# Attention and two MLPs on one core: zero products ahead of the loop, an earlier load of v, six score buffers, and where the weight conversion stands

## The chip, the cores and the metric

The kernel runs on one core of one Trainium2 chip. The core has TensorE (PE; PEld is its weight load), VectorE (DVE), ScalarE (ACT), GpSimd (POOL) and SyncE (SP, which here only issues transfers). The metric is device time in microseconds (us), lower is better. Of three runs of the kernel before the median is 755.74 us (747.38 to 756.08).

## The reference

Attention over two batches ("halves" b = 0 and 1), 12 heads, 448 tokens, with a 12x12 mixing of the heads before and after the softmax, and behind it two MLPs on all 896 tokens.

```python
scores = scale * np.matmul(q, k.transpose(0, 1, 3, 2))
scores = np.einsum('bhij,hg->bgij', scores, w_pre)
attn = np.exp(scores - np.max(scores, axis=-1, keepdims=True))
attn = attn / (np.sum(attn, axis=-1, keepdims=True) + 1e-09)
attn = np.einsum('bhij,hg->bgij', attn, w_post)
x = np.matmul(attn, v)            # to (896, 768)
x = ((x @ w_a) * (x @ w_b)) @ moe_w_out
out = np.maximum(x @ w_in, 0.0) ** 2 @ moe2_w_out
```

All of it is in fp32; `moe_` and `moe2_` weights are 768x1536, 1536x768, 768x2048 and 2048x768.

## The kernel before

The 448 query rows of a half are cut into four tiles of 120, 120, 120 and 88 rows (`tiles`, t = 0 to 3), eight tiles in all. For each pair of heads c = 0 to 5 a tile's scores are made on TensorE by `qk` (L188, products at L201), copied from PSUM (`qk_copy`, L208: odd heads on VectorE, even heads on ScalarE), and each head's copy is spread by a transfer (`spread`, L215, mostly issued on SP) into `G`, in which the 12 heads of a query row lie on neighbouring partitions. There are two `G`, one for even and one for odd t. From the third tile on the copies land in `s` buffers, four of them before (L113); a buffer is free again when the spread that reads it has landed.

The loop (L705) runs over 46 slots. A slot takes one or two groups of ten query rows (`PAIRS`); tiles have 6, 6, 6, 5, 6, 6, 6 and 5 slots, so tiles begin at slots 0, 6, 12, 18, 23, 29, 35 and 41 (`base`). In slot n TensorE mixes the heads of slot n+1 (`premix`, L287, T from G), then does the second mixing of slot n (`post`, L336). The softmax of n+1 is a minimum on VectorE (L296), an exponential on ScalarE (L303) and, in `weights2`, three small VectorE steps (L315 to L317) that fold 1/sum into the weights of `post`. `evac` (L353 VectorE, L355 ScalarE) copies the result of `post` into `a`. In the last slot of a tile the product with v follows (`av`, L367, six head pairs in three thirds; each third is copied by `av_out`, L377, on VectorE).

Everything else is put into slots by lists: `mid`, `end`, `pre`, `aft` and `dve_l` hold calls by slot. The scores of the next tile are called in six successive slots from three before the current tile's start. The load of v for half two (`load_v`, 1344 KB) is called at slot 20. A weight unit is 768 columns of 128 rows, 68 units in all; it is loaded on SP (`load_w`, L489) and converted in six steps, s0 to s5 (L497 to L532): s0 to s3 on VectorE (L503, L507, L514, L518; s0 with a ScalarE step, L502), s4 on ScalarE (L524), and s5 the low part, on GpSimd for units 0 and 1 (`lower`, L163) and on VectorE for the rest (L531). Eighteen steps, three units, are called one by one in slots 31 to 42 through `dve_l`, right behind `weights2`.

In front of the loop the scores of tile 0 are made and spread, even heads from GpSimd's queue and odd heads from SP's (`hw`, L406; `first_out`, L418); the first slot has a path of its own (`direct`). Nine products with a zero column (`busy`, L396) fill the time in which the first inputs load. Behind the loop the dense part (`stage`, L594) does the MLPs, three products per 128x128 block of weights. Its first 11 block steps are called inside slots 41 to 45 (`fill`).

Of the kernel before, what the change touches and what calls it, by code (L numbers as in the profile page):

```python
# [40 lines left out]
R0 = 2 * ND  # L41
# [27 lines left out]
def attention_moe_kernel(  # L69
# [22 lines left out]
    def rd(ap):  # L92
        return ap.bitcast(F32)
# [18 lines left out]
    sb = att.enter_context(tc.tile_pool(name="att", bufs=1))  # L112
    s_p = att.enter_context(tc.tile_pool(name="s", bufs=4))  # L113
    e_p = att.enter_context(tc.tile_pool(name="e", bufs=2))
# [303 lines left out]
    def first_out():  # L418
        while Sps:
            _, t, h, p = Sps.pop(0)  # L420
            qk_copy(ROWS0, h, p, stage0[h])
            spread(0, h, stage0[h], R0, H, hw[h % 2])

# [14 lines left out]
    NS = len(plist)  # L438
    dve_l, pre, aft, mid, end = {}, {}, {}, {}, {}

    def at(d, slot, *f):
        d.setdefault(max(slot, 0), []).append(f)
# [5 lines left out]
    for ti, (b, t) in enumerate(tiles):  # L448
        s0, sp = base[ti], span[ti]
        if ti + 1 < len(tiles):  # L450
            nxt = tiles[ti + 1]
            for c in range(NC):
                if ti:
                    at(mid, s0 - 3 + c, qk, *nxt, c)
# [15 lines left out]
        if ti + 1 < len(tiles):  # L470
            for c in range(NC):
                at(end, s0 + sp - 1, av, b, t, c)
                if c % 2:
                    at(end, s0 + sp - 1, av_out, b, t, c // 2)
        if t == 1 and b + 1 < B:
            at(mid, s0 + sp + 8, load_v, b + 1)

# [4 lines left out]
    whl = {}  # L482
    todo = []

# [9 lines left out]
    def split_steps(u):  # L494
# [31 lines left out]
        def s5():  # L526
            lo = w_p.tile([128, UW], F32R, tag="wl", name="wl", bufs=3)
            if u < 2:
                lower(lo, st["c"], st["hi"], 6)
            else:  # L530
                nc.vector.tensor_tensor(out=lo, in0=st["c"], in1=rd(st["hi"]), op=ALU.subtract)  # L531
            whl[u] = (st["hi"], lo)  # L532
# [3 lines left out]
    def split_w(u):  # L536
        if u < NU:
            todo.extend(split_steps(u))

    def steps(n):  # L540
        for _ in range(min(n, len(todo))):
            todo.pop(0)()

# [16 lines left out]
    s1 = base[-2]  # L560
    at(mid, s1 - 8, load_w, 0)
    at(mid, s1 - 8, load_w, 1)
    for u in range(3):
        at(mid, s1 - 5, split_w, u)
    for i in range(18):
        at(dve_l, s1 - 4 + (2 * i) // 3, steps, 1)
    for c in range(NC):
# [130 lines left out]

    premix(*plist[0])
    softmax(0)  # L700
    qk(0, 1, 0)
# [3 lines left out]
    for n in range(NS):  # L705
# [12 lines left out]
        if n + 1 < NS:  # L718
            weights2(*plist[n + 1])
        run(dve_l, n)  # L720
        run(mid, n)
# [116 lines left out]
```

## Time and profile before

| | |
|---|---|
| median of 3 runs | 755.74 us (747.38 to 756.08) |
| the profiled execution | 758.59 us, span 756.8 us |
| its mean granted TensorE clock | 0.979 |
| TensorE busy | 728.2 us, 96% of the span |
| VectorE, ScalarE, GpSimd busy | 483.7, 309.5, 83.0 us |
| HBM read | 62.29 MB, 86 GB/s over the span |

The profile was taken in one execution of its own. All times in its rows are us from the start of the span. A row of the order in time gives the start, the busy time of a merged run of instructions, the engine, the line, the operation, what it writes and reads, and in brackets how long the engine was idle before and what ended that. The granted clock is a share of 2.4 GHz.

### The profile page before, as it was taken

The page shows a single profiled execution, that of the slowest core. Times are in us where ns is not written, and L with a number is a line of the kernel's source. Part 1 is how long each engine was busy: PE and PEld are TensorE (multiplying, and loading weights), DVE is VectorE, ACT ScalarE, POOL GpSimd, SP SyncE. Part 2 cuts the span into 40 slices and gives each one's busy share as a digit, 9 for nine tenths or more (in the row PEclk, how much of TensorE's full clock was granted, in tenths as well). Part 3 has the DMA queues.
Part 4 walks back from the last instruction along what each step waited for, and adds up shares of the span by engine and source line. Part 5 has one row for each costly group of instructions (what it writes and reads, how often), then busy time and mean ns, then how long its engine had stood idle before and what let it go on. Part 6 is the DMA issues. An engine that isn't in the chain of part 4 may idle for free.

```text
span 756.8 us, 13175 instructions
## 1 busy us (share of the span) xinstructions
PE 728.2 (96%) x5309; PEld 611.4 (81%) x5309; DVE 483.7 (64%) x820; ACT 309.5 (41%) x581; POOL 83.0 (11%) x181
## 2 busy tenths in 40 slices
PE   8799996999989999999999999999999999999998
PEld 2466773776667899999999999999999999999997
DVE  6467664568665576676667755656888888544440
ACT  3358644546544433333333333324555554332220
POOL 4126721102840000000000000000000000000000
PEclk9799998899979999999999999999999999999999
DMA  7564336263310133323322332332232323443410
GB/s 231 147 187 147 107 102 186 73 212 129 109 61 2 43 122 101 112 84 126 123 86 92 121 121 84 126 123 86 85 126 85 124 90 120 149 147 112 134 40 25
DMA packets 27451, 84.75 MB, mean 112 GB/s; under 512 B 4422, under 2 KB 16890, under 8 KB 27166
## 3 DMA queue, kind: packets, MB, share of 16 engines
q1 hardware_dynamic: 24286, 80.08, 32.3%
q0 software_dynamic: 2528, 2.75, 1.4%
q10 hardware_dynamic: 576, 1.07, 0.4%
q8 instruction: 42, 0.69, 0.4%
q14 instruction: 19, 0.16, 0.1%
HBM read 62.29 MB, written 2.75 MB: 86 GB/s over the span
## 4 chain that ended last, share of the span: by engine, by line
PE 83%; DMA 6%; DVE 3%; issue 3%; POOL 2%; ACT 2%; SPq 0%; DVEq 0%; ACTq 0%; POOLq 0%
PE T L574 8%; PE T L575 8%; PE T L573 8%; PE post L336 6%; PE qk L573 6%; PE post L575 6%; PE post L573 6%; PE post L574 6%; PE qk L575 5%; PE qk L574 5%; DMA G<-s 4%; PE av L367 3%; PE T L287 3%; PE av L575 3%; PE av L574 3%; PE av L573 3%
## 5 line engine op out<-in xcount | busy, mean ns | idle before, releaser
L336 PEld LDWEIGHTS post<-w,e 64*112 64x112 f32 x1440 | 80.9, 182 | 36.0 <-issue 21.9
L524 ACT CAST wh<-wc 128x768 fp32r<-128x768 f32 x68 | 56.8, 835 | 121.8 <-DVE wc L518 108.8
L531 DVE TENSOR_TENSOR wl<-wc,wh 128x768 fp32r<-128x768 f32 x66 | 63.0, 955 | 49.6 <-ACT wh L524 49.6
L336 PE MATMUL post<-w,e 64*112 64x60 f32 x1440 | 86.2, 268 | 4.5 <-DVE w L317 4.1
L303 ACT ACTIVATE e<-T,nb 128x448 f32<-128x448 f32 (+1 forms) x92 | 57.5, 630 | 77.4 <-DVE nb L296 77.4
L574 PE MATMUL T<-m,wh 128*128 128x448 f32 x213 | 78.5, 368 | 0.2 <-DVE m L549 0.2
L573 PE MATMUL T<-m,wh 128*128 128x448 f32 x213 | 78.5, 368 | 0.0
L575 PE MATMUL T<-m,wl 128*128 128x448 f32 x213 | 78.4, 368 | 0.0
L507 DVE SCALAR_TENSOR_TENSOR wa<-wr,wa 128x768 uint32<-128x768 uint32 x68 | 65.3, 961 | 2.3
L518 DVE SCALAR_TENSOR_TENSOR wc<-wc,wa 128x768 uint32<-128x768 uint32 x68 | 65.2, 958 | 2.2
L287 PE MATMUL T<-G,wpre_sb 64*64 64x448 f32 x352 | 49.8, 587 | 12.4 <-DMA G<-s 7.0
L502 ACT ACTIVATE wc<-wr 128x768 f32<-128x768 f32 x68 | 61.6, 906 | 0.0
L296 DVE TENSOR_REDUCE nb<-T 128x1 f32<-128x448 f32 (+1 forms) x92 | 52.9, 615 | 13.4 <-PE T L287 13.0
L514 DVE TENSOR_SCALAR wc<-wc 128x768 f32<-128x768 f32 x68 | 37.7, 555 | 16.6 <-ACT wc L502 16.6
L573 PE MATMUL post<-m,wh 128*128 128x448 f32 x125 | 46.0, 368 | 0.0
L574 PE MATMUL post<-m,wh 128*128 128x448 f32 x125 | 46.0, 368 | 0.0
L575 PE MATMUL post<-m,wl 128*128 128x448 f32 x125 | 46.0, 368 | 0.0
L353 DVE COPY a<-post 112x480 f32<-112x480 f32 x44 | 30.1, 684 | 24.9 <-PE post L336 24.9
L574 PEld LDWEIGHTS T<-m,wh 128*128 128x128 f32 x213 | 40.0, 188 | 4.6 <-DVE m L549 0.5
L573 PEld LDWEIGHTS T<-m,wh 128*128 128x128 f32 x213 | 40.0, 188 | 4.3 <-ACT m L548 0.3
L575 PEld LDWEIGHTS T<-m,wl 128*128 128x128 f32 x213 | 40.0, 188 | 4.0
L573 PE MATMUL qk<-m,wh 128*128 128x448 f32 x116 | 42.7, 368 | 0.0
(163 smaller groups left out, 1454.1 us busy)
## 6 DMA issues: line engine op xcount, KB each, us to landing
wr<-w SPq DMA_DIRECT2D x68, 768.0 KB
G<-s SPq DMA_DIRECT2D x44, 210.0 KB
G<-s SPq DMA_DIRECT2D x22, 140.0 KB
k<-kT SPq DMA_DIRECT2D x12, 224.0 KB
v<-v SPq DMA_DIRECT2D x2, 1344.0 KB
outT<-ta SPq DMA_DIRECT2D x12, 224.0 KB
q<-qT SPq DMA_DIRECT2D x6, 360.0 KB
G<-x POOLq DMA_DIRECT2D x6, 175.0 KB, 5.4
```

The source lines that it names most:

```text
L287: nc.tensor.matmul(p[f][o:o + 64, 0:S], wpre_sb[i:i + 64, o:o + 64], G[t % 2][i:i + 64, r + g, :], start=True, stop=True, skip_group_check ...
L296: nc.vector.tensor_reduce(out=NB[b, m][0:q, f:f + 1], in_=Tps[b, m][f][0:q, 0:S], op=ALU.min, axis=AX.X)
L303: nc.scalar.activation(out=e[0:q], in_=Tps[b, m][f][0:q, 0:S], func=ACTF.Exp, bias=NB[b, m][0:q, f:f + 1], scale=-1.0, accum_out=Z[b, m][0 ...
L336: nc.tensor.matmul(p[g][0:JP, c:c + k], e[o:o + 64, j * JP:(j + 1) * JP], w2[o:o + 64, f, :], start=True, stop=True,)
L502: nc.scalar.activation(out=st["c"], in_=rd(st["high"]), func=ACTF.Abs, scale=HSC)
L507: nc.vector.scalar_tensor_tensor(out=a, in0=st["high"], scalar=0x80000000, in1=a, op0=ALU.bitwise_and, op1=ALU.bitwise_or)
L518: nc.vector.scalar_tensor_tensor(out=cu, in0=cu, scalar=3, in1=st["a"], op0=ALU.logical_shift_left, op1=ALU.bitwise_or)
L524: nc.scalar.copy(st["hi"], st["c"])
L531: nc.vector.tensor_tensor(out=lo, in0=st["c"], in1=rd(st["hi"]), op=ALU.subtract)
L573: nc.tensor.matmul(p[:, 0:S], hi[:, sl], x[0], start=first, stop=False)
L574: nc.tensor.matmul(p[:, 0:S], hi[:, sl], x[1], start=False, stop=False)
L575: nc.tensor.matmul(p[:, 0:S], lo[:, sl], x[0], start=False, stop=last)
```

## The change

- `busy(16)` is called between `premix` and `softmax` of the first slot: 16 more zero products.
- In front, the spreads of heads 8 and 10 of tile 0 are issued by ScalarE and not by GpSimd.
- `s` has six buffers and not four.
- `load_v` for half two moves from slot 20 to slot 17 (the last slot of a tile).
- Of the scores of half two's first tile, head pair 3 moves to the end of slot 17, behind the product with v, and pairs 4 and 5 follow one slot sooner (slots 18 and 19).
- `dve_l` is gone. The weight steps are called at slots 28, 34 and 40 only, between the thirds of the product with v: 2+2, 2+2+3 and 2+2+1 steps (`STEPS`); the last two of the eighteen come in `attention_tail`. Units 0 and 1 are loaded at slots 22 and 28 (both at 27 before). The low part of units 0 and 1 is made by VectorE.

```diff
-    s_p = att.enter_context(tc.tile_pool(name="s", bufs=4))
+    s_p = att.enter_context(tc.tile_pool(name="s", bufs=6))
...
-            spread(0, h, stage0[h], R0, H, hw[h % 2])
+            spread(0, h, stage0[h], R0, H, nc.scalar if h in (8, 10) else hw[h % 2])
...
+    STEPS = ((2, 2, 0), (2, 2, 3), (2, 2, 1))
...
-                if ti:
+                if ti == 3:
+                    if c != 3:
+                        at(mid, s0 - 3 + c - (c > 3), qk, *nxt, c)
+                elif ti:
                     at(mid, s0 - 3 + c, qk, *nxt, c)
...
                 if c % 2:
+                    if b:
+                        at(end, s0 + sp - 1, steps, STEPS[t][c // 2])
                     at(end, s0 + sp - 1, av_out, b, t, c // 2)
-        if t == 1 and b + 1 < B:
-            at(mid, s0 + sp + 8, load_v, b + 1)
+        if ti == 2:
+            at(end, s0 + sp - 1, qk, *tiles[4], 3)
+        if t == 2 and b + 1 < B:
+            at(mid, s0 + sp - 1, load_v, b + 1)
...
-            if u < 2:
-                lower(lo, st["c"], st["hi"], 6)
-            else:
-                nc.vector.tensor_tensor(out=lo, in0=st["c"], in1=rd(st["hi"]), op=ALU.subtract)
+            nc.vector.tensor_tensor(out=lo, in0=st["c"], in1=rd(st["hi"]), op=ALU.subtract)
...
-    at(mid, s1 - 8, load_w, 0)
-    at(mid, s1 - 8, load_w, 1)
+    at(mid, base[4] - 1, load_w, 0)
+    at(mid, base[5] - 1, load_w, 1)
     for u in range(3):
-        at(mid, s1 - 5, split_w, u)
-    for i in range(18):
-        at(dve_l, s1 - 4 + (2 * i) // 3, steps, 1)
+        at(mid, base[5] - 1, split_w, u)
...
     premix(*plist[0])
+    busy(16)
     softmax(0)
```

ScalarE's order in front of the loop, where the copies of the last heads of tile 0 stand (`x` are the copies, `G_83` is the `G` of even tiles, x_1_122 and x_2_123 are heads 8 and 10):

```order
 L266 COPY s<-T 128x448
 L212 COPY x_1_122<-qk 100x448
+L220 DMA G_83<-x_1_122 10x10x448
 L212 COPY x_2_123<-post 100x448
+L220 DMA G_83<-x_2_123 10x10x448
 L303 ACTIVATE e,z<-T,nb 128x448 x2
 L212 COPY v_124<-qk 120x448
```

The two transfers now stand on ScalarE between the copies and the first exponentials; they were in GpSimd's queue.

SP's queue around the spreads of half two's first tile and of the tile after it (`G_83` and `G_84` are the two `G`; `wr` is a weight unit):

```order
 L220 DMA G_83<-s 10x12x448 x2
 L140 DMA q<-qT 128x720
-L220 DMA G_83<-s 10x12x448 x8
+L220 DMA G_83<-s 10x12x448 x2
 L184 DMA v<-v 112x3072
-L220 DMA G_83<-s 10x12x448
+L220 DMA G_83<-s 10x12x448 x7
 L220 DMA G_83<-s 9x12x448
 L223 DMA G_83<-s 1x12x448
 L220 DMA G_84<-s 10x12x448 x2
 L140 DMA q<-qT 128x720
```

The load of v stood behind ten of the tile's spreads and stands behind four now.

VectorE's order in slot 28, the last slot of half two's first tile. Before:

```order
L317 TENSOR_TENSOR w_2093<-wp,z 128x120
L210 COPY s<-qk 120x448
L377 COPY x_0_2124<-av 128x2x120
L377 COPY x_1_2143<-post 128x2x120
L377 COPY x_2_2162<-av 128x2x120
L296 TENSOR_REDUCE nb<-T 128x1 x2
```

With the change (L516, L520, L527 and L531 of the changed kernel are L503, L507, L514 and L518 before):

```order
L317 TENSOR_TENSOR w_2108<-wp,z 128x120
L210 COPY s<-qk 120x448
L516 TENSOR_SCALAR wa<-wr 128x768
L520 SCALAR_TENSOR_TENSOR wa<-wr,wa 128x768
L377 COPY x_0_2148<-av 128x2x120
L527 TENSOR_SCALAR wc<-wc 128x768
L531 SCALAR_TENSOR_TENSOR wc<-wc,wa 128x768
L377 COPY x_1_2169<-post 128x2x120
L377 COPY x_2_2188<-av 128x2x120
L296 TENSOR_REDUCE nb<-T 128x1 x2
```

The first four steps of unit 0 came between the product with v and its copies; in slots 31 to 33, where they stood behind L317, they are gone.

## Rows read from the trace of the kernel before

**Rows 1.** Busy time by stretch: engines (instructions), clock, DMA share, GB/s.
```profile
20.00:30.00 10.00, 7.10 (x46) 4.71 (x48) 2.09 (x4) 2.13 (x6) 0.78 (x2) 0.61 0.46 123
130.00:140.00 10.00, 10.00 (x104) 7.92 (x104) 2.88 (x8) 2.88 (x7) 0.00 (x0) 0.59 0.33 104
220.00:230.00 10.00, 9.06 (x108) 8.03 (x106) 2.88 (x8) 1.17 (x4) 0.00 (x0) 0.65 0.20 75
290.00:300.00 10.00, 10.00 (x50) 9.09 (x49) 7.34 (x11) 3.29 (x6) 0.00 (x0) 1.00 0.26 80
```

**Rows 2.** Order in time, slots 17 to 23: start, busy, engine, line, idle before.
```profile
100.53 0.53 ACT L212 COPY s<-qk 120x448 f32<-120x448 f32 x1 [1.36 <-DMA G<-s]
...
108.87 1.78 PE L336 MATMUL post<-w,e 64*112 64x60 f32 x32
...
115.49 1.78 PE L336 MATMUL post<-w,e 64*112 64x60 f32 x32
...
117.90 0.49 SPq L184 DMA_DIRECT2D v<-v  x1
...
121.12 1.79 PE L336 MATMUL post<-w,e 64*112 64x60 f32 x32
...
129.74 2.12 PE L287 MATMUL T<-G,wpre_sb 64*64 64x448 f32 x8 [6.17 <-DMA G<-s]
...
131.79 2.87 PE L336 MATMUL post<-w,e 64*112 64x60 f32 x14
...
141.87 1.78 PE L336 MATMUL post<-w,e 64*112 64x60 f32 x32
```

**Rows 3.** Order in time, slots 32 to 41.
```profile
177.51 1.78 PE L336 MATMUL post<-w,e 64*112 64x60 f32 x32
...
190.18 1.86 PE L367 MATMUL av<-a,v 112*64 112x120 f32 x32 [0.93 <-ACT a L355]
...
193.73 0.41 DVE L377 COPY x<-post 128x240 f32<-128x240 f32 x1 [1.23 <-PE post L367]
...
195.25 0.98 PE L287 MATMUL T<-G,wpre_sb 64*64 64x448 f32 x8
...
214.79 1.59 DVE L315 TENSOR_SCALAR z<-z 128x2 f32<-128x2 f32 x1
...
221.22 3.47 PE L367 MATMUL av<-a,v 112*64 112x120 f32 x32 [0.94 <-ACT a L355]
...
229.09 0.98 PE L287 MATMUL T<-G,wpre_sb 64*64 64x448 f32 x8
...
231.43 1.78 PE L336 MATMUL post<-w,e 64*112 64x60 f32 x32
```

**Rows 4.** Order in time, front: zero products, first wait, first and third `post`.
```profile
0.93 3.52 PE L399 MATMUL av<-warm 128*1 128x448 f16 x9 [0.93 <-DVE warm L381]
...
22.90 2.03 PE L287 MATMUL T<-G,wpre_sb 64*64 64x448 f32 x8 [4.66 <-DMA G<-x]
...
26.50 3.11 PE L336 MATMUL post<-w,e 64*112 64x60 f32 x32
...
36.86 1.78 PE L336 MATMUL post<-w,e 64*112 64x60 f32 x32
```

**Rows 5.** Order in time: the first two VectorE steps of a weight unit.
```profile
177.29 0.55 DVE L503 TENSOR_SCALAR wa<-wr 128x768 uint32<-128x768 uint32 x1
...
177.88 0.96 DVE L507 SCALAR_TENSOR_TENSOR wa<-wr,wa 128x768 uint32<-128x768 uint32 x1
```

**Rows 6.** The chain of work that ended last: start, us, what.
```profile
15.72 7.05 DMA G<-x
...
35.22 0.80 PE qk L201 x4
...
139.81 1.21 PE av L367 x32
```

**Rows 7.** The page's DMA issues: count, KB each, median us to landing.
```profile
G<-x POOLq DMA_DIRECT2D x6, 175.0 KB, 5.4
```

More of the change, by code (lines that the diff above doesn't have):

```diff
@@ L438, in attention_moe_kernel, with steps @@
     NS = len(plist)
-    dve_l, pre, aft, mid, end = {}, {}, {}, {}, {}
+    pre, aft, mid, end = {}, {}, {}, {}
+    STEPS = ((2, 2, 0), (2, 2, 3), (2, 2, 1))
+    todo = []
+    def steps(n):
+        for _ in range(min(n, len(todo))):
+            todo.pop(0)()
     def at(d, slot, *f):
@@ L482, in attention_moe_kernel @@
     whl = {}
-    todo = []
     def load_w(u):
@@ L538, in split_w @@
             todo.extend(split_steps(u))
-    def steps(n):
-        for _ in range(min(n, len(todo))):
-            todo.pop(0)()
     xs = [[None] * NC for _ in range(B)]
@@ L719, in attention_moe_kernel @@
             weights2(*plist[n + 1])
-        run(dve_l, n)
         run(mid, n)
```

## The prediction

> **What bounds the kernel now.** I read the table by stretch first [rows 1]. From about 253 us to the end TensorE is busy 10.00 us of every 10 at the full granted clock (1.00, 2.4 GHz), with VectorE at some 7: the reader sees one row of it, and the rows up to 740 us are like it. This is the dense part; the change does not touch its products, so its 504 us stay. Everything to be won lies in the 253 us of attention. There the table has three bad stretches, 20 to 30 us (clock 0.61), 130 to 140 (0.59, behind a long wait) and 220 to 230 (0.65). In each the clock has fallen to its lower level, 1.2 GHz, after TensorE had little to do.
>
> Next I read the order in time. One trip of the loop, a slot, runs from one `post` product (L336) to the next, so the starts of L336 give the length of each slot. An undisturbed slot takes 3.3 us (108.87 to 115.49 is two of them) [rows 2]. A slot that ends a tile also holds the product with v, and takes about 8.7: 1.78 for `post`, 0.9 for scores, 5.07 for the product (190.18 to 195.25), 0.98 for the next mixing product [rows 3]. Lengths above these are the loss, and they lie in three places.
>
> Front: TensorE has done the scores of tile 1 that it can at 18.24 and waits 4.66 us for the spread of scores into `G`; the eight products behind that wait take 2.03 us, against 0.98 later [rows 3, 4]. Middle: slots 20 to 22, 115.49 to 141.87, in which a `G<-s` transfer behind the 1.3 MB load of v ends a wait of 6.17 us [rows 2]. End of attention: slots 32 to 40, 177.51 to 231.43, where the steps of weight conversion stand in VectorE's queue between one slot's softmax and the next [rows 3, 5].
>
> **The change, part by part.** The sum is made against the profiled execution, 758.59 us with a span of 756.8; the median of the runs shown is 755.74, 2.85 below it.
>
> *Front.* Sixteen zero products go in behind the first mixing product. Nine of them took 3.52 us at half clock, 0.39 each [rows 4]; the trace has none at full clock, so the price lies between 0.39 each (6.3 us in all) and half of it (3.1). I take 3.1, since the clock stood at 1.00 where they go; half clock was seen only after the wait. They start at 16.5 and end near 19.6, and the two score products that now follow them (0.8 to 1.0 each [rows 6]) end near 21.6. The wait is then filled to within 1.3 us, if `G` comes when it did. It was ended by a spread issued on SP at 15.72 that took 7.05 us to land, while tile 1's first four spreads were already under way [rows 6]. These now start 3 us later, and the spreads of heads 8 and 10 leave POOL's queue (5.4 us to landing [rows 7]) for ACT's. So I take `G` to be there at about 21.5. ACT issues two more transfers ahead of its exponentials, some 0.8 us each by SP's spreads; the first `post` comes 3 us after these are done, so that is covered. At full clock the slots then run: mixing 0.98 and scores 0.85, `post` at 23.4 instead of 26.50; two further slots of 4.8 (with two score products each waiting for the copies of the one before) and 3.6 us, so the third `post` at 31.8 instead of 36.86 [rows 4]. **Front: 5.0 us saved.** If `G` comes no sooner than 22.90, 3.7. If the zero products don't hold the clock, they only delay scores that nobody waits for yet: 0. Above, if `G` lands by 20.5, the score products still end at 21.6, so 5.3.
>
> The Trainium skill, DMA: Bandwidth & Descriptors, section "Issuing engines are not separate DMA queues", says that the queues of SP, ACT and POOL feed the same 16 DMA engines. By it heads 8 and 10 would land no sooner for leaving POOL, and the front would save the 3.7 and not the 5.0; no row of the kernel before has a spread on ACT's queue, so this stays open.
>
> *Middle.* Two things move. The load of v goes from slot 20, where SP issued it at 117.90 among the last spreads of the tile, to slot 17, whose product with v gives its transfer 5 us in which few others are due. And the scores of heads 6 and 7 are made one slot sooner, so the last spread leaves in slot 20 and not in 21, two slots ahead of the mixing product that reads it. That product then has no wait: slot 20 shrinks from 5.63 to 3.3, slot 21 from 10.67 to 3.3, and slot 22 (half a `post`, the 88-row product with v at 1.21 for each third [rows 6], full clock) from 10.08 to 6.8: 12.98 saved [rows 2]. The moved score product costs slot 17 its 0.85. Six `s` buffers let the copies run three score products ahead of the landing; ACT's wait of 1.36 us for `G<-s` in slot 17 [rows 2] is one of two in a row on the chain there, and I count 1.2 for them. **Middle: 13.0 - 0.85 + 1.2 = 13.4.** Bounds: 6 if the load now delays the spreads of slots 17 and 18 by its own 5 us and half the wait comes back; 14.5 at best. What is queued behind the load on SP are those spreads, and who waits for them is the copy three score products later.
>
> *End of attention.* In slots 31 to 42 eighteen steps leave VectorE's queue between softmaxes. A unit costs VectorE 0.55 and 0.96 in its first pair of steps [rows 5], two instructions of the same shape again, and one such for the low part: some 4 us. They now stand between the thirds of the product with v in slots 28, 34 and 40, where VectorE waits 1.23 us before each copy of 0.41 [rows 3]. Cover: a window of 5.07 us, less three copies of 0.41 and one of 0.62, leaves 3.2 for the 3.0 of steps in slot 28; slot 34 has 4.0 for the 3.2, and overruns by 0.8, of which the next mixing product (0.98) and `post` hide most. The low parts of two units go from POOL to VectorE, 0.96 each, inside the 4.0. Two steps are left for the last product with v; the dense part has 25 product triples before it reads that unit. So the nine slots 32 to 40 become seven of 3.4 (the casts of x stay), one of 8.8, and the last: 1.78, 0.9 of wait for a copy, 5.07, and 2.34 from its mixing product to the next `post` (229.09 to 231.43), 10.1 [rows 3]. That is 42.7 against 53.92: **11.2 saved**; the half clock of 217 to 227 us is in it. Bounds: 8 if all three windows overrun by 1 us; 13 if the slots go at 3.3 and overrun nothing.
>
> A row beside it: z's step on two columns took 1.59 us at 214.79, while POOL subtracted [rows 3]. The Trainium skill, SBUF — State Buffer, section "Who interferes with whom", says that the one of the two engines that comes second to their shared port blocks fully until the other is done. By it, the POOL subtractions of x that stay could still block such steps, and if that took 0.3 in each of six slots the end would save 9.4; the row agrees, but it stands beside a POOL subtraction of weights, which goes.
>
> **Sum:** 5.0 + 13.4 + 11.2 = 29.6, so 758.6 - 29.6 = 729.0 for a profiled execution; the unprofiled runs of the kernel before stand 2.85 lower, which gives 726.2. I say 727.
>
> **The rivals.**
> 1. *The load of v only moves its collision.* Spreads of slots 17 and 18 land 5 us late and stop the copies in spite of six buffers; the middle saves 6 and not 13.4: 734. For it: 6.17 us of wait followed this very load. Against: in slot 17 the product with v goes on for 5 us in which no copy is due.
> 2. *The clock falls at another place.* Half speed made 3.47 us of a third of the product with v at 221.22, which takes 1.86 at 190.18 [rows 3]; over such a fall that is 4 to 5 us: 732. Against: all three falls followed a wait or thin slots that go away.
> 3. *The steps overrun, and `G` is late in front.* VectorE late by 1 us in each window (end 8.2), zero products without effect (front 0): 735.
> 4. *Little comes.* Front 0, middle 6, end 8: 741.7, within 2%. It needs three lower bounds at once.
> 5. *Slower.* Unit 2 is finished only in the tail. If the line of units stays one behind through the dense part, TensorE waits at each of its 68 units: 0.44 us a unit eats the 29.6, and from 0.65 (44 us, 771) the kernel is slower by 2%. Against: VectorE is busy only 7 of 10 us there [rows 1], so it catches up within a few units.
>
> **How the numbers follow.** Forecast with all three savings near their size: 0.64, own range 721 to 733. Rival 1: 0.12; rival 2: 0.10; rival 3: 0.07; rival 4: 0.05; rival 5: 0.02. The range takes in the best bounds (5.3 + 14.5 + 13 = 32.8, so 723, and a little more for the offset of 2.85) and rivals 1 to 3 above: 720 to 736. A measurement of this kernel can tell about 2% from no change, 15 us: faster than 740.6 are the forecast and rivals 1 to 3, 0.93; within 2% rival 4 and half of rival 5, 0.06; slower 0.01.
>
> **What would show it.** Right: granted clock 1.00 in all stretches from 10 to 240 us; the first `post` of the loop near 23.4; no wait above 1 us for `G<-s` near 110 us; slots 29 to 40 at 3.3 to 3.5 us except where the product with v stands; the dense part from about 223. Wrong: a fall of the clock at 20 us, a wait of TensorE in the middle of the product with v in slots 28, 34 and 40, or waits for `wl` after the start of the dense part.

## The result

The changed kernel takes 721.23 us (median of four runs, 719.91 to 725.20) against 755.91 us before (747.38 to 757.57); the ratio is 0.9572, 95% interval 0.9490 to 0.9653. It is faster, as forecast, and the forecast of 727 lies 5.8 us above it. Two errors of opposite sign make that small difference, and the sections below are about them. The profiled execution of before, 758.59 us, is one of the longer ones of its kernel (747.38 to 757.57 in the other four).

The profiled execution of the changed kernel takes 725.20 us, with a span of 723.4. Its table by stretch, with the columns of [rows 1] (engines' busy time, clock, DMA share, GB/s):

```profile
20.00:30.00 10.00, 10.00 (x104) 5.82 (x103) 6.68 (x16) 5.69 (x15) 2.84 (x5) 1.00 0.56 147
...
40.00:50.00 10.00, 7.88 (x101) 5.78 (x99) 5.01 (x14) 5.09 (x14) 3.11 (x8) 0.91 0.75 214
...
130.00:140.00 10.00, 9.95 (x140) 6.80 (x141) 8.30 (x21) 7.58 (x19) 2.43 (x6) 1.00 0.29 87
...
220.00:230.00 10.00, 9.97 (x156) 8.81 (x154) 3.05 (x8) 3.22 (x9) 0.00 (x0) 1.00 0.01 2
```

The three bad stretches of before, at clocks of 0.61, 0.59 and 0.65, are at 1.00. A new one has come, 40 to 60 us (0.91 in its first half, 0.92 in its second). TensorE's order in time shows where it comes from (start, busy, line, idle before):

```profile
17.65 3.22 PE L399 MATMUL av<-warm 128*1 128x448 f16 x16
...
22.49 0.98 PE L287 MATMUL T<-G,wpre_sb 64*64 64x448 f32 x8
...
24.25 1.69 PE L336 MATMUL post<-w,e 64*112 64x60 f32 x32
...
32.05 1.78 PE L336 MATMUL post<-w,e 64*112 64x60 f32 x32
...
47.07 2.40 PE L367 MATMUL av<-a,v 112*64 112x120 f32 x32 [1.88 <-DMA v<-v]
49.19 3.04 PE L367 MATMUL post<-a,v 112*64 112x120 f32 x32
```

Against [rows 4], the wait of 4.66 us in front is gone, sixteen zero products took 3.22 us, and the third `post` starts at 32.05 instead of 36.86. Then, at 47.07, the product with v waits 1.88 us for the load of half one's v; the clock falls, and its second third takes 3.04 us where such a third takes 1.81 to 1.86 elsewhere.

The middle and the end of attention, in the same view:

```profile
114.59 1.78 PE L336 MATMUL post<-w,e 64*112 64x60 f32 x32
...
121.69 0.98 PE L287 MATMUL T<-G,wpre_sb 64*64 64x448 f32 x6 [0.32 <-DMA G<-s]
122.60 1.58 PE L336 MATMUL post<-w,e 64*112 64x60 f32 x14
...
129.88 1.29 PE L336 MATMUL post<-w,e 64*112 64x60 f32 x22
...
165.39 1.78 PE L336 MATMUL post<-w,e 64*112 64x60 f32 x32
...
200.30 1.86 PE L367 MATMUL av<-a,v 112*64 112x120 f32 x32 [0.88 <-DVE z L315]
...
207.70 1.49 PE L336 MATMUL post<-w,e 64*112 64x60 f32 x26
```

The wait of 6.17 us for `G<-s` [rows 2] has become 0.32 in this trace, and slots 32 to 40 run from 165.39 to 207.70, 42.31 us, instead of 53.92 [rows 3].

Starts of `post` (L336) cut each trace into the same stretches. Before and after were both profiled a second time, on one chip (the runs e_before and e_after below), and the table has all four traces, in us:

| stretch | before, 1st | after, 1st | saved | before, 2nd | after, 2nd | saved |
|---|---|---|---|---|---|---|
| start to slot 6 | 55.73 | 54.71 | 1.02 | 52.76 | 51.73 | 1.03 |
| slots 6 to 15 | 39.72 | 39.96 | -0.24 | 39.46 | 40.34 | -0.88 |
| slots 16 to 23 | 49.74 | 38.54 | 11.20 | 51.79 | 37.36 | 14.43 |
| slots 24 to 31 | 32.32 | 32.18 | 0.14 | 32.20 | 32.18 | 0.02 |
| slots 32 to 40 | 53.92 | 42.31 | 11.61 | 52.79 | 42.31 | 10.48 |
| slot 41 to the end | 525.37 | 515.70 | 9.67 | 515.70 | 515.68 | 0.02 |
| span | 756.8 | 723.4 | 33.4 | 744.7 | 719.6 | 25.1 |

Three lines were not foreseen: the first, where only 1.0 of the 4.8 us won by the third `post` is left; the second, where the changed kernel loses (0.24 and 0.88); and the last but one, where the first pair of traces shows 9.67 us that the second does not.

### The profile page after: what moved, and what is told of

The parts are those of the page before. It is cut to its first block, busy times and chain, and to the rows that moved or that the text cites. A ratio compares the mean times of both kernels' runs of the same rounds, so it can differ in the third digit from the quotient of the medians.

```text
span 723.4 us, 13184 instructions
## 1 busy us (share of the span) xinstructions
PE 708.0 (98%) x5325; PEld 604.4 (84%) x5325; DVE 482.8 (67%) x822; ACT 309.1 (43%) x581; POOL 76.9 (11%) x167
## 4 chain that ended last, share of the span: by engine, by line
PE 88%; DMA 4%; POOL 2%; DVE 2%; issue 2%; ACT 1%; SPq 0%; DVEq 0%; ACTq 0%; POOLq 0%
PE T L578 9%; PE T L579 9%; PE T L577 9%; PE post L336 7%; PE qk L577 6%; PE post L577 6%; PE post L579 6%; PE post L578 6%; PE qk L579 6%; PE qk L578 6%; PE T L287 4%; PE av L367 3%; PE av L577 3%; PE av L578 3%; PE av L579 3%; PE qk L201 2%
## 5 line engine op out<-in xcount | busy, mean ns | idle before, releaser
L336 PEld LDWEIGHTS post<-w,e 64*112 64x112 f32 x1440 | 76.9, 175 | 32.8 <-issue 14.0
L541 DVE TENSOR_TENSOR wl<-wc,wh 128x768 fp32r<-128x768 f32 x68 | 65.3, 960 | 48.5 <-ACT wh L537 48.5
L336 PE MATMUL post<-w,e 64*112 64x60 f32 x1440 | 82.1, 260 | 2.7 <-DVE w L317 2.2
L520 DVE SCALAR_TENSOR_TENSOR wa<-wr,wa 128x768 uint32<-128x768 uint32 x68 | 65.3, 960 | 2.3
L531 DVE SCALAR_TENSOR_TENSOR wc<-wc,wa 128x768 uint32<-128x768 uint32 x68 | 65.2, 958 | 2.3
L527 DVE TENSOR_SCALAR wc<-wc 128x768 f32<-128x768 f32 x68 | 37.7, 555 | 14.7 <-ACT wc L515 14.7
L287 PE MATMUL T<-G,wpre_sb 64*64 64x448 f32 x352 | 45.6, 561 | 1.1 <-issue 0.8
```

The lines of the kernel that those rows point to most:

```text
L287: nc.tensor.matmul(p[f][o:o + 64, 0:S], wpre_sb[i:i + 64, o:o + 64], G[t % 2][i:i + 64, r + g, :], start=True, stop=True, skip_group_check ...
L336: nc.tensor.matmul(p[g][0:JP, c:c + k], e[o:o + 64, j * JP:(j + 1) * JP], w2[o:o + 64, f, :], start=True, stop=True,)
L520: nc.vector.scalar_tensor_tensor(out=a, in0=st["high"], scalar=0x80000000, in1=a, op0=ALU.bitwise_and, op1=ALU.bitwise_or)
L531: nc.vector.scalar_tensor_tensor(out=cu, in0=cu, scalar=3, in1=st["a"], op0=ALU.logical_shift_left, op1=ALU.bitwise_or)
```

## The experiments

In each short diff, - stands for what is taken out and + for what is put in. Beside each experiment the kernel before was timed on the same chip, and ratios are to that.

### Before and after once more: whose are the 9.67 us?

No edit in either.

> The kernel before, unchanged, profiled a second time. It is here for the dense part, from 253 us on. In the first trace of before its products start 206.67 ns apart, in the trace of after 202.67 ns apart, at a granted clock of 1.00 in both; over 2448 products that is 9.8 us, which no part of the change accounts for. Theory A (the spacing belongs to the execution and not to the kernel): 202.67 or 206.67 can come out, and with 202.67 the time is near 746, where one of the runs of before (747.38) lies. Theory B (the spacing belongs to the kernel): 206.67 again and a time of 755 to 758. One trace with 206.67 leaves both standing; one with 202.67 ends B. The 253 us ahead of the dense part should be as they were, within 1 us, by both.

> The changed kernel, unchanged, profiled a second time. Theory A (spacing of the dense products belongs to the execution): 202.67 or 206.67 ns; with 206.67 the time is near 730, with 202.67 near 720. Theory B (it belongs to the kernel): 202.67 and 720 to 722. Front: in the first trace the product with v at the end of slot 5 waited 1.88 us for the load of v at 47 us, the clock fell for 3.4 us, and 3.8 of the 4.8 us won in front were lost. Theory C (this belongs to the changed kernel: its front is shorter, and the load of v, issued at 33.9, shares the engines with the spreads): the wait is there again, and slot 6 starts near 54.7. Theory D (it was that run, whose inputs came 1 us later than those of before): no wait above 0.5 us near 47, no fall, and slot 6 starts near 51.

Measured: e_before 746.52 us (one run); before, timed beside it, has a median of 751.0 (745.04 to 760.56, 13 runs). e_after 723.5 us (721.03 to 731.82), ratio 0.9674, interval 0.9602 to 0.9747. Below are four rows of the same product (units' high part times the input) in the dense part, one each of before in its first trace, of e_before, of the changed kernel in its first trace, and of e_score_move (a run told of below); min, median and max of a product's record in ns, then first and last start in us:

```profile
L573 PE MATMUL T<-m,wh x149: 368/368/368, 302.8 to 696.5; 128*128 128x448 f32 x149
```
```profile
L573 PE MATMUL T<-m,wh x158: 362/365/369, 300.0 to 698.9; 128*128 128x448 f32 x158
```
```profile
L577 PE MATMUL T<-m,wh x166: 362/365/369, 300.1 to 697.2; 128*128 128x448 f32 x166
```
```profile
L578 PE MATMUL T<-m,wh x154: 368/368/368, 309.8 to 699.7; 128*128 128x448 f32 x154
```

There are two kinds of execution: one in which every record is 368 ns and the products start 206.67 ns apart, and one with 362 to 369 ns and 202.67 ns apart on the mean. The granted clock is 1.00 in both. Before is of the first kind in its first trace and of the second in its second. Theory B falls: the kernel does not set it, and the 9.67 us of the first comparison are no gain of the change. With equal spacing the change is worth 25.1 us of span in this one pair of traces, and 27.5 by the medians taken beside them (751.0 - 723.5); e_before is one of the shorter executions of before.

On the front, e_after has the collision again, in a milder form: theory C is right about the place and too high in size, slot 6 starts at 51.73 and not at 54.7, and the clock stays at 1.00. The waits, in its order in time:

```profile
41.41 1.10 PE L287 MATMUL T<-G,wpre_sb 64*64 64x448 f32 x8 [1.32 <-DMA v<-v]
...
45.75 1.86 PE L367 MATMUL av<-a,v 112*64 112x120 f32 x32 [0.71 <-DMA v<-v]
```

The first of the two reads only what the spreads of tile 1 wrote; the profile names the load of v, beside which these spreads ran. The landing of a spread is in the trace as the last update of its semaphore: the last spread of tile 1, issued on SP at 31.84, has landed at 41.15, and the product starts at 41.41. So the mixing product of slot 4 is late, and then the product with v in slot 5: 4.94 and 9.29 us against 3.43 and 8.74 in before. The third `post` started at 30.81 against 33.89; 2.05 of these 3.08 us are lost here.

The same happens once more in slot 10, whose mixing product is the first to read tile 2:

```profile
68.52 1.29 PE L287 MATMUL T<-G,wpre_sb 64*64 64x448 f32 x8 [0.81 <-issue]
```

The last spread of tile 2 landed at 68.70, and in e_before the same product starts at 68.72. So by slot 16 only 0.15 us of the front's gain is left in the second pair of traces, and 0.78 in the first.

### The front alone, and the end alone

```
+    busy(16)                                       # behind premix(*plist[0])
-    spread(0, h, stage0[h], R0, H, hw[h % 2])
+    spread(0, h, stage0[h], R0, H, nc.scalar if h in (8, 10) else hw[h % 2])
```

> The kernel before with the front of the change alone: sixteen zero products behind the first mixing product, and the spreads of heads 8 and 10 on ACT's queue. If the savings of the parts add: third post near 32.0 instead of 36.86. Theory C (the load of v collides because the front is shorter): a wait of TensorE of 1 to 2 us for v near 47 us, slot 6 near 54.7 and 1.0 us saved in all, so 754.9 at the 206.67 spacing. Theory D (the collision was that run's): slot 6 near 51 and 4.8 us saved, 751.1. A rival by which zero products only hold up the scores behind them: third post at 36 or later and nothing saved, 756. Theory B on the spacing (the change makes it): it stays at 206.67 unless this part carries it; theory A: either value.

Measured: ratio 0.9963, interval 0.9929 to 0.9997 (747.75 us against 751.0). Third `post` at 30.74, slot 4 at 5.00 us and slot 5 at 9.27, slot 6 at 51.70, where e_before has 52.76: 1.06 us saved. That is less than traces of one front differ by: the six with the front of before have the third `post` at 33.89 to 36.86 and slot 6 at 52.76 to 55.73, the three with the changed one (after, e_after, e_front) 30.74 to 32.05 and 51.70 to 54.71. The wait is that of the changed kernel (1.38 us ahead of the mixing product of slot 4), so the shorter front brings it about by itself, and theory D falls.

The end alone is the changed kernel with the edits of the front and the middle taken back.

> The kernel before with the end of the change alone: weights loaded earlier, their conversion taken between the thirds of the product with v in slots 28, 34 and 40, the low parts of units 0 and 1 on VectorE. If the savings add and this one is its own: slots 32 to 40 take 42.3 us instead of 53.92, everything ahead of slot 24 stays, 11.6 us saved, 744.3 at the 206.67 spacing and 734.5 at 202.67. Rival (part of it came from the middle, whose stall moved the end of the tile against the loads): 6 to 8 us saved, with a wait for a weight load or a spread above 1 us in slots 24 to 40. Rival 5 of the prediction (units one behind in the dense part): waits of TensorE for wl after 245 us.

Measured: 735.07 us, ratio 0.9794, interval 0.9734 to 0.9855. Slots 32 to 40 take 42.73 us against 52.79 in e_before, in its order in time:

```profile
175.77 1.78 PE L336 MATMUL post<-w,e 64*112 64x60 f32 x32
...
218.50 1.69 PE L336 MATMUL post<-w,e 64*112 64x60 f32 x30
```

10.06 us are saved, so this part stands alone. Span 734.3 against 744.7; the medians differ by 15.9, e_before being shorter than most executions of before. No wait of TensorE for `wl` follows; rival 5 of the prediction has nothing for it.

### Which half of the front did what

Zero products out of the changed kernel:

```
-    busy(16)
```

> The changed kernel without its sixteen zero products (the spreads of heads 8 and 10 stay on ACT's queue). If the zero products keep TensorE's clock up in front (the prediction's step): the wait ahead of the mixing product near 21 us is 2 us or more, the granted clock falls below 1.00 within 20 to 35 us, and the third post starts 1.5 to 3 us later than the 30.81 and 32.05 us of the changed kernel, at 33 to 34. Rival (the spreads on ACT's queue did all of it): third post within 0.5 us of 31, clock 1.00. By the time of slot 6 (51.7 us in the second trace of the changed kernel) little or nothing is left of either, if the load of v is what slots 4 and 5 wait for: 51.5 to 53, and the time within 1.5 us of the changed kernel's.

The heads back on POOL's queue in the changed kernel:

```
-    spread(0, h, stage0[h], R0, H, nc.scalar if h in (8, 10) else hw[h % 2])
+    spread(0, h, stage0[h], R0, H, hw[h % 2])
```

> The changed kernel with the spreads of heads 8 and 10 back on POOL's queue (the zero products stay). If the queue matters (the prediction's step): G comes later, a wait ahead of the mixing product near 21 us of 1 to 2.5 us, third post 1 to 2.5 us later than 30.81, at 32 to 33.3. By the Trainium skill, DMA: Bandwidth & Descriptors, section 'Issuing engines are not separate DMA queues', the queue should not matter: third post within 0.4 us of 30.81. Slot 6 near 51.7 by both, if slots 4 and 5 wait for the load of v.

Measured, without zero products: the third `post` at 35.24 (a miss: later than expected), slot 6 at 54.11 (a miss, by 1.1 us), span 722.0, 724.05 us (ratio 0.9652, 0.9606 to 0.9698). Order in time and table by stretch:

```profile
21.27 1.89 PE L287 MATMUL T<-G,wpre_sb 64*64 64x448 f32 x8 [2.58 <-DMA G<-x]
...
24.73 3.11 PE L336 MATMUL post<-w,e 64*112 64x60 f32 x32
```
```profile
20.00:30.00 10.00, 8.73 (x52) 4.87 (x56) 4.36 (x11) 3.49 (x9) 1.74 (x3) 0.54 0.58 158
```

The wait of 2.58 us is back and the clock is at 0.54: the zero products do hold it up, and that is worth 4.4 us at the third `post` (35.24 - 30.81). At slot 6 it is worth 2.4 against e_after, since slots 4 and 5 of this kernel take their 3.43 and 8.75: what comes later collides less. Against the first trace of the changed kernel (slot 6 at 54.71) nothing is left, and the times show no gain from the zero products either: 0.9652 stands beside 0.9674 for the changed kernel, with intervals that overlap.

With the heads on POOL's queue the third `post` comes at 31.77, 0.96 us later, between the two expectations; the time is 726.05 us (ratio 0.9705, 0.9667 to 0.9743). In its order in time there is a wait ahead of the first mixing product from `G` again:

```profile
22.10 1.10 PE L287 MATMUL T<-G,wpre_sb 64*64 64x448 f32 x8 [0.67 <-DMA G<-x]
```

So the move to ACT's queue brings about 1 us in front. The two traces of the changed kernel differ by more, 1.24 us, but there the first mixing product (L279) itself starts 1.24 us apart: counted from it, the third `post` comes 16.05 us later in all three traces with the changed front and 16.91 here. The Trainium skill, DMA: Bandwidth & Descriptors, section "Issuing engines are not separate DMA queues", says that issuing on several engines saves no more than the time it takes to issue, as all transfers run on the same 16 engines. The traces do not agree: ACT issues heads 8 and 10 in e_after at 14.71 and 17.00, no sooner than POOL here (15.04 and 15.79), and yet `G` is complete later here. What lands last here is not a spread of POOL (21.31) but SP's, issued at 16.59 and landed at 21.92; in e_after SP's, issued at 16.48, has landed at 19.74. Counted from the first mixing product, `G` is complete after 5.61 to 5.85 us in the five traces with these heads on ACT and v loaded at its place (e_nozero among them, at 5.76), and after 6.75 to 8.21 in the seven with them on POOL (7.06 here). So the queue alone brings `G` sooner, with or without zero products; why SP's last spread lands later beside POOL's stays open.

Slot 6 was a miss (53.70 instead of 51.7): its product with v waited 1.63 us. Beyond their 12.17 us slots 4 and 5 lose 2.06 us in e_after, 3.07 here and 3.81 in the first trace of the changed kernel, so the collision varies from trace to trace by some 2 us.

### Where the front's gain went

Half one's v loaded earlier, in the changed kernel:

```
+    load_v(0, nc.scalar)        # behind the last first_out()
-    at(mid, 2, load_v, 0)
```

> The changed kernel with one move more: the load of half one's v is issued on ACT's queue behind the spread of head 10 (near 18 us), instead of on SP's queue in slot 2 (33.4 us). In the traces of the changed kernel and of the front alone, the 16 DMA engines carry next to nothing at 20 to 22 us and are full from 33 to 42 us, where the mixing product of slot 4 waits 1.3 us and the product with v 0.7 us (1.88 in the first trace). Theory E (the engines are full because v comes among the spreads of tile 1): with v in the gap, slots 4 and 5 take 3.43 and 8.74 again, slot 6 starts 2.0 us earlier against the third post than in the changed kernel, near 49.6, and 2 us are saved: about 721.4 against 723.5 where the changed kernel stands there. Rival F (the bytes only move): the spreads of tile 0 or tile 1 land later for it, the third post comes 1 to 3 us later, and nothing is saved. Rival G (the spreads of tile 1 alone fill the engines): slot 4 still 4.9.

Measured: the wait for v in slot 5 is gone (8.73 us), but slot 4 still takes 4.81, and slot 6 starts at 51.05 and not at 49.6. Rival G is right about slot 4, theory E about slot 5; 0.7 us are won there, and the median (724.13 us, ratio 0.9676, 0.9625 to 0.9727) shows no gain. What slot 4 waits for is `G` of tile 1, whose last spread, issued at 31.83, landed at 41.09 (the transfer that the profile names goes to the other `G`, on the same queue), in TensorE's order in time:

```profile
41.28 1.10 PE L287 MATMUL T<-G,wpre_sb 64*64 64x448 f32 x8 [1.19 <-DMA G<-s]
```

So the place of v's load does not decide slot 4. In the changed kernel the zero products stand ahead of tile 1's first scores, so all its spreads start late. The next run turns these two round:

```
-    busy(16)
     softmax(0)
     qk(0, 1, 0)
+    busy(16)
```

> The changed kernel with the first score product of tile 1 (heads 0 and 1) ahead of the sixteen zero products instead of behind them. The prediction counted the later scores at nothing, since nobody waits for them yet. Theory J (they cost the front's gain: the spreads of tile 1 start at 21.3 us instead of 18.2, the DMA engines idle at 20 to 22 us, and the same bytes then hold up the mixing product of slot 4 and the product with v in slot 5): with two heads' spreads in the gap, 0.43 MB of the 200 KB that pass in a us, slots 4 and 5 lose 1 to 2 us less; slot 6 near 50 to 50.8 against 51.73 if the first mixing product comes when it did, and 51 to 51.7 if the spreads of tile 0 now land up to 1 us later for it. Rival K (the zero products' place does not matter, slot 4 waits for the last spread issued, at 31 to 33 us): slots 4 and 5 still 4.9 and 9.3, slot 6 at 51.7 or later.

Measured: 719.88 us (719.66 to 720.09, four runs), ratio 0.9607, interval 0.9562 to 0.9652, span 717.9. Third `post` at 31.27; then, in TensorE's order in time,

```profile
40.47 0.98 PE L287 MATMUL T<-G,wpre_sb 64*64 64x448 f32 x8
41.38 1.78 PE L336 MATMUL post<-w,e 64*112 64x60 f32 x32
...
44.15 1.86 PE L367 MATMUL av<-a,v 112*64 112x120 f32 x32 [0.18 <-ACT a L355]
...
50.13 1.78 PE L336 MATMUL post<-w,e 64*112 64x60 f32 x32
```

with no wait of note in slots 4 and 5 (3.43 and 8.75 us) and slot 6 at 50.13, 1.60 us ahead of the changed kernel's second trace and 2.63 ahead of e_before, which is the earliest there of the six traces with the front of before. The table by stretch shows why, two rows of the changed kernel (e_after) and then two of e_scores; the last two columns are DMA share and GB/s:

```profile
20.00:22.00 2.00, 2.00 (x16) 0.58 (x12) 1.28 (x5) 1.06 (x2) 0.23 (x1) 1.00 0.01 4
33.00:42.00 9.00, 7.12 (x96) 4.32 (x88) 6.45 (x18) 6.17 (x16) 2.81 (x8) 1.00 1.00 230
```
```profile
20.00:22.00 2.00, 2.00 (x13) 0.66 (x14) 0.30 (x2) 0.18 (x1) 0.58 (x1) 1.00 0.56 158
33.00:42.00 9.00, 8.44 (x110) 4.97 (x110) 7.18 (x19) 6.62 (x17) 2.37 (x7) 1.00 0.93 243
```

With the zero products first, the DMA engines stand still for 2 us (share 0.01), and later all sixteen are full for 9 us, while TensorE waits; with the scores first, the gap carries 158 GB/s, and the later stretch, though it moves more (243 GB/s against 230), is no longer full. How long the six spreads of tile 1 that POOL issues take to land (min, median, max in us), in e_after and then in e_scores:

```profile
DMA to landing us min/median/max: 4.0/7.8/9.6
```
```profile
DMA to landing us min/median/max: 3.0/5.4/7.0
```

The last spread of tile 1 is issued later in e_scores, at 32.30 against 31.84, and lands sooner, at 37.78 against 41.15. So theory J holds, and rival K, by which its issue sets the wait, falls. This kernel has the lowest median of all that were run. Against the changed kernel the 1.7 us of span are shown by one pair of traces; the two ratios to before, 0.9607 and 0.9674, have intervals that overlap.

Three moves at once did not add up:

```
     (the turn of e_scores, and the early load of e_v_early)
-        if t == 2 and b + 1 < B:
-            at(mid, s0 + sp - 1, load_v, b + 1)
+        if ti == 1:
+            at(mid, s0 + 1, load_v, 1)
```

> The changed kernel with three moves: the first score product of tile 1 ahead of the zero products, half one's v on ACT's queue behind the spread of head 10, and half two's v loaded in slot 7 (55 to 60 us, where the DMA engines have a share of 0.28) instead of slot 17 (97 us, 0.87 to 0.98 in the 10 us behind it). If the front is bound by bytes (theory J): slots 4 and 5 at 3.43 and 8.74, slot 6 near 49.7 to 50.5; slot 10 at 3.5 as with v early. If the load of half two's v still makes the last spreads of its tile late in slot 21 (3.29 in one trace of the changed kernel, 4.57 in the other, 4.71 with v early): slot 21 at 3.3. Sum 2 to 4 us against the changed kernel's 719.6 us of span: 716 to 718. Rival L (v and the scores of tile 1 together hold up the spreads of tile 0): a wait of 1 to 3 us ahead of the mixing product near 21 us, and a span of 719 to 721.

Measured: 736.06 us, ratio 0.9808 (0.9745 to 0.9871), span 736.0: 18 to 20 us above the first expectation and 15 to 17 above rival L's. Slot 3 takes 9.46 us and slot 10 takes 10.98 (3.43 and 4.45 in e_after), and slot 11, at half clock, 12.07. Order in time, and a row of the table by stretch:

```profile
40.35 1.85 PE L201 MATMUL qk<-k,q 64*120 64x448 f32 x4 [4.19 <-DMA q<-qT]
...
78.99 1.89 PE L287 MATMUL T<-G,wpre_sb 64*64 64x448 f32 x8 [6.75 <-DMA q<-qT]
```
```profile
40.00:42.00 2.00, 1.65 (x4) 0.48 (x4) 0.00 (x0) 0.00 (x0) 0.00 (x0) 0.50 0.07 25
```

In slot 3 TensorE waits for a load of q that was issued at 25.14 us, while at the end the DMA share is 0.07, about one engine of sixteen (0.0625). A likely reading is that one engine was left far behind by the large packets of v; it was not tried apart. It does not cover slot 10: that product reads no q, and the last spread of tile 2, issued at 68.45 behind the load of half two's v (61.67), landed at 78.98, with a share of 0.94 from 76 to 78 us. Slot 21 did come out at 3.29, but it does so in e_after too, with that load in slot 17.

### The middle, in parts

The load of half two's v alone, in the kernel before:

```
-        if t == 1 and b + 1 < B:
-            at(mid, s0 + sp + 8, load_v, b + 1)
+        if t == 2 and b + 1 < B:
+            at(mid, s0 + sp - 1, load_v, b + 1)
```

> The kernel before with the load of half two's v alone moved, from slot 20 to slot 17; the scores of heads 6 and 7 and the four s buffers stay as they were. Two halves of the middle's saving (11.2 us by the first two traces, 14.4 by the second two, over slots 16 to 23) are told apart. Theory H (the load was the cause of the wait): the wait of some 6 us for G<-s ahead of the mixing product in slot 21 goes, and slots 16 to 23 take 38 to 42 us instead of 49.7 and 51.8. Rival (the last spread leaves too late by itself): that wait stays at 2 us or more, slots 16 to 23 take 43 to 47. Rival 1 of the prediction (with four buffers the load now stops the copies of slots 17 and 18): slot 17 or 18 longer by 2 to 5 us.

Measured: slots 16 to 23 take 41.56 us, 10.2 less than in e_before, with slot 21 at 5.25 and slot 22 at 7.29; 739.34 us, ratio 0.9900 (0.9838 to 0.9961). Theory H holds in size, but 1.64 us of idle time stay ahead of the mixing product in slot 21. Slots 17 and 18 are no longer than before (9.35 and 3.32), so rival 1 falls. Slot 20 stays at 5.66: it holds two score products, and the second waits for ACT's copy of the first, which stands behind the exponentials in ACT's queue and waits for no buffer. Two rows of its order in time for slot 20, one for slot 21:

```profile
116.28 0.54 ACT L212 COPY s<-qk 120x448 f32<-120x448 f32 x1
...
116.87 0.46 PE L201 MATMUL qk<-ks,qh 64*120 64x448 f32 x1 [0.87 <-ACT s L212]
...
123.30 1.23 PE L287 MATMUL T<-G,wpre_sb 64*64 64x448 f32 x8 [1.64 <-issue]
```

The whole middle in the kernel before (the kernel of this run moves the load too, though its text says that it stays):

```
     (the load's move of e_v2, s_p with bufs=6, and)
+        if ti == 2:
+            at(end, s0 + sp - 1, qk, *tiles[4], 3)
```

> The kernel before with six s buffers and the scores of heads 6 and 7 of half two's first tile one slot sooner; the load of half two's v stays in slot 20. The load's move alone made slots 16 to 23 take 41.6 us instead of the 51.8 of the second trace of before: slot 21 5.25 and slot 20 still 5.66. The whole middle takes 37.4 (38.5 in the first trace of the changed kernel). If the two parts add: 2.5 to 4.2 us saved here, slot 20 at 3.4, the wait for G<-s behind the load of v still there in slot 21 (10 to 11 us), slots 16 to 23 at 47.5 to 49.5. Rival (either part alone cures the wait, since the last spread now leaves ahead of the load): slot 21 at 3.3 to 5.3, slots 16 to 23 at 38 to 42.

Measured: slots 16 to 23 take 37.61 us, as in the changed kernel (37.36 and 38.54); 737.57 us, ratio 0.9839 (0.9766 to 0.9912). Its slots 32 to 40 take 56.49 us, longer than the 52.79 and 53.92 of before, so part of the gain is lost there; why stays open. As to what it was to tell apart it decides nothing; the last run does:

```
     (e_mid without the load's move)
```

> The kernel before with six s buffers and the scores of heads 6 and 7 of half two's first tile one slot sooner, and with the load of half two's v left in slot 20. (The kernel of the run e_mid moved that load too: it is the whole middle of the change, and its text tells of it wrongly.) In SP's queue the load now stands behind all spreads of its tile, not ahead of the last of them. Slots 16 to 23 took 51.8 us in before, 41.6 with the load's move alone, 37.6 with all three. Theory M (the wait in slot 21 is for that last spread, behind the load, and either part takes it away): slot 20 at 3.4 (5.6 with the load's move alone, where four buffers and the later scores stay), slot 21 at 3.3 to 5, slots 16 to 23 at 37.5 to 40; half two's v, read only in slot 28, costs nothing there. Theory N (the load shares the engines with spreads already issued, wherever it stands in SP's queue near them, so its own move is needed): slot 21 at 6 to 11, slots 16 to 23 at 41 to 49.

Measured: slots 16 to 23 take 38.25 us; 740.36 us, ratio 0.9859 (0.9802 to 0.9916). Slot 20 takes 3.43 and slot 21 4.29; order in time:

```profile
118.06 1.98 PE L287 MATMUL T<-G,wpre_sb 64*64 64x448 f32 x8
...
119.03 0.23 PEld L287 LDWEIGHTS T<-G,wpre_sb 64*64 64x64 f32 x6 [0.79 <-ACT s L212]
...
119.97 1.58 PE L336 MATMUL post<-w,e 64*112 64x60 f32 x14
```

Theory M holds: of the wait of 6 us there is left that the mixing product takes 1 us longer than its 0.98, as the weights of its later parts are loaded 0.79 us late, and that with the load of v where it always was. The scores' move and the two buffers (not told apart) save 13.5 us alone, the load's move 10.2, both together 14.2 to 14.4, all against e_before, the longest here of the four traces with the middle of before (49.74 to 51.79): they cure the same wait. By its ratio each of the three kernels lies within 2% of before (0.9839 to 0.9900).

## Why the prediction was right, and where not

**Total.** The sum was 29.6 us; the spans of the first pair differ by 33.4, of the second pair by 25.1. The time of 727 came out 5.8 us high because, as far as the traces tell, before ran mostly with the wide spacing in that comparison and the changed kernel with the narrow one (one trace of each; the other executions have none).

**"So their 504 us stay."** This step failed for the first comparison: 9.67 us came from the spacing of products that nobody changed. The one run of 747.38 beside 755.74 and 756.08 stood in the times of before, 8.4 us below the others, and the prediction made nothing of it. In the second pair the dense part stays to within 0.02 us.

**Front, 5.0.** The mechanism was right up to the third `post`: forecast 31.8, measured 32.05 and 30.81; the clock held at 1.00, and without zero products it falls to 0.54. `G` was complete at 21.61 and 20.61, forecast 21.5, and the heads' queue, credited for it, is what brought it. The price of 3.1 for sixteen zero products was right (3.22, 0.20 each); that the first nine, at 0.39 each, ran at half clock is not in before's table by stretch, which has 1.00 from 0 to 10 us. The step that failed is the price of the scores held up behind the zero products, nothing: the prediction says of them that "nobody waits for yet", and the sum has no term for them. The copies and spreads of these scores feed the DMA engines, and slots 4, 5 and 10 wait for what lands late for it. Of 5.0 us, 1.0 is left at slot 6 and 0.15 to 0.78 at slot 16. With the order turned (e_scores) 2.6 are left at slot 6 against e_before. Rival 2, a fall of the clock at another place, came true in the first trace (40 to 60 us, 0.91 and 0.92) and not in the second, so the sign "granted clock 1.00 in all stretches" was met in one of the two.

**Middle, 13.4.** Measured 11.20 and 14.43, inside the bounds of 6 and 14.5. Slots 20 and 22 came out near their forecasts (3.44 and 7.29 to 7.39, against 3.3 and 6.8); the term that varies is slot 21, forecast 3.3 and measured 4.57 and 3.29, where one trace waits for its last spread and the other does not. The prediction credited load and scores together; either one alone takes away most of the wait. Rival 1 did not happen.

**End, 11.2.** Measured 11.61 and 10.48, and 10.06 by itself. The windows of the product with v hold the steps as counted: slot 34 takes 8.88 and slot 40 takes 10.06, forecast 8.8 and 10.1. This is not safe from rival 2: in two of the eight traces with this end, e_heads and e_all, the clock falls in the last product with v (0.83 from 200 to 210 us in e_heads, behind the usual short wait), and slot 40 takes 11.7:

```profile
199.60 2.97 PE L367 MATMUL av<-a,v 112*64 112x120 f32 x32 [0.87 <-DVE z L315]
```

The step on two columns, 1.59 us at 214.79 [rows 3], takes no more than 0.2 in slots 32 to 40 of the changed kernel (view of one line: min, median, max in ns, first and last start in us):

```profile
L315 DVE TENSOR_SCALAR z<-z x9: 149/155/203, 168.1 to 200.0; 128x2 f32<-128x2 f32 x9
```

The POOL subtractions of x are still there, and the loss of 0.3 a slot did not come, which the prediction took as a case for the rule of the Trainium skill, SBUF — State Buffer, "Who interferes with whom" (of two engines at their shared port the second blocks until the first is done); the one long step of before is gone together with the weight subtractions on POOL.

**What was hit by luck.** The time lies near the forecast because the front was put 4 us too high and the dense part, by the first pair of traces, 9.7 us too low. Taken by the second pair, the forecast saving of 29.6 is 4.5 above the measured 25.1: 4.0 of that is the front up to slot 6, 0.9 the loss in slots 6 to 15, 0.7 the end, and the middle came out 1.0 better than forecast.

## What to carry to other kernels

Put filler that keeps TensorE's clock up behind whatever starts transfers (worth 1.6 us at slot 6 here, in one pair of traces): work that "nobody waits for yet" may be the source of the bytes that everybody waits for 20 us later, so look for an empty stretch in the DMA share ahead of a full one. Two edits that cure one wait must not be added up; undo each alone. And where the runs of one kernel fall into two groups, profile it again before reading a difference between two kernels, above all one in a part that the change does not touch.

## What the chip showed that was not expected

The same products, at a granted clock of 1.00, start 206.67 ns apart in some executions and 202.67 ns apart in others, constant within each from 260 us to the end; over the dense part that is 9.7 us, 1.3% of the kernel. Of fourteen traces two have the wide spacing (before, first trace, and e_score_move, whose profiled execution took 743.31 us while others of the same kernel took 734.08, 737.42 and 748.45). What decides it stays open.

Before's own front varies too: its first slot takes 7.02 us in the first trace and 4.19 in e_before, after waits of 4.66 and 4.52 us, as the clock falls in the one for longer (0.61 from 20 to 30 us) than in the other (0.83). With the zero products it took 4.19 in every one of seven traces. The wait in e_before:

```profile
22.73 1.98 PE L287 MATMUL T<-G,wpre_sb 64*64 64x448 f32 x8 [4.52 <-DMA G<-x]
```
